# Opening of a transformer block on one core: block 0's chain first, four tokens to a partition, and block 1's query passes drawn between the opening's last steps

## Chip, cores and metric

The kernel runs on one core of one Trainium2 chip. The metric is the device time of an execution in microseconds. TensorE is PE in the profile (its weight loads PEld), VectorE is DVE, ScalarE is ACT, GpSimd is POOL; SyncE, which issues the transfers, is SP.

## What is computed

A pre-norm transformer block on x of 2048 tokens by 576 features: multi-query attention with 32 heads of 18 features and a single key and value head, then a gated bilinear feed-forward layer of 4608 features. All arrays are float32.

```python
def _A_ref(x, wq, wk, wv, wo):            # B, S, D = 1, 2048, 576; H, Dh = 32, 18
    q = (x @ wq).reshape(B, S, H, Dh).transpose(0, 2, 1, 3)
    k = x @ wk
    v = x @ wv
    scores = einsum("bhqd,bkd->bhqk", q, k) * (Dh ** -0.5)
    o = einsum("bhqk,bkd->bhqd", softmax(scores, axis=-1), v)
    return o.transpose(0, 2, 1, 3).reshape(B, S, H * Dh) @ wo
def _B_ref(x, w_gate, w_up, w_down):      # F = 4608
    return ((x @ w_gate) * (x @ w_up)) @ w_down
h = x + _A_ref(_layernorm(x), wq, wk, wv, wo)
out = h + _B_ref(_layernorm(h), w_gate, w_up, w_down)
```

## The kernel before

The 2048 tokens are four blocks of 512, each of four tiles of 128 tokens. Nearly every operand of PE is split in a high and a low part, and a product is the sum of three: high by high, high by low, low by high. A projection over 576 features is therefore 14 matmuls of 512 columns (`passes`), of which four need only the high parts and four the low part of x.

`keys_values` is the opening. It is written out by hand: the order of its lines is the order in each engine's queue. For every block it loads x, takes the layer norm's statistics (`stats`, DVE), makes scales (`scale`: an inverse root by three Newton steps on the engine it is given, `rstd`), normalises (`apply`, ACT), transposes on PE (`turn`: two PSUM tiles of the kind `ps_s` and a tail), and splits the transposed block into `XT` (`parts`: ACT casts the high part, DVE subtracts the low one). Then it projects keys, values and the last four query heads (`project`, tile `psk`), and writes keys to `kT` (`keys`) and values to `V` (`values`). For block 0 it also projects the other 28 query heads in four groups of seven (`query`, tile `psq`; `ready` splits and stores them in `q_dram`). `bound` and `bounds` make a row m for each head that bounds its scores from above: DVE's `tq` is the queries' size, `psg` the matmul, and m goes through `m_dram`. It is computed at first for group 0 alone, with `G0`.

Attention works in pairs. `pair` (L533, L534) is two score matmuls into one of the two `ps_s` tiles and one exponential on ACT, which makes P. `flush` (L538) adds two pairs' P times V into `acc`, one matmul for each of four heads. A step is two pairs and one flush; block 0 has 256 pairs, and each later block too. The transposes of the opening and the scores take turns in the same two `ps_s` tiles.

After `keys_values`, the loop in `run` draws the queries of blocks 1 to 3 (`queries`; one pass is one matmul of each of the two half-arrays `psq` and `psr`, L389) between the pairs at `RATE` = 1.9 a step, until none is left. `blocks` goes on: bare steps in which POOL and DVE split the output weights, steps with pieces of block 0's output projection (`outs`, tile `yo`, L689, three matmuls a piece, one or two pieces a step), the feed-forward layer of block 0 (`ffn`, L925) with pairs of later blocks between its matmuls, and so on. The places around the change:

```python
def apply(b, lo=0, hi=NQ):
    for s in range(lo, hi):
        ...
        act.activation(xh, xs[b][:, s, :], AF.Identity, bias=n, scale=r)
...
self.outs(2 if len(self.yos) > 1 else 1)
```

Of the kernel before, what the change touches and what calls it, by code (L numbers as in the profile page):

```python
# [54 lines left out]
class Block:  # L55
# [9 lines left out]

    def ps_s(self, name):
        return self.ps.tile([P, 2, TB], F32, tag="s", bufs=2, name=name)
# [34 lines left out]
    def rstd(self, var, name, eng=None, n=NQ):  # L102

        dve = eng or self.dve
        v = self.lp.tile([P, n], F32, tag="v", name=f"v{name}")
        t = self.lp.tile([P, n], F32, tag="t", name=f"t{name}")
        y = self.lp.tile([P, n], F32, tag="y", name=f"y{name}")
        yi = self.lp.tile([P, n], I32, tag="yi", name=f"yi{name}")
        dve.tensor_scalar(v, var, 1e-5, None, ALU.add)
        dve.tensor_copy(t, v.bitcast(I32))  # L110
        dve.tensor_scalar(yi, t, -0.5, 1597463007.0, ALU.mult, ALU.add)
        dve.tensor_scalar(v, v, -0.5, None, ALU.mult)
        g = yi.bitcast(F32)
        for _ in range(3):
            dve.tensor_tensor(t, g, g, ALU.mult)
            dve.tensor_tensor(t, t, v, ALU.mult)
            if eng is self.nc.gpsimd:
                eng.tensor_scalar(t, t, 1.5, None, ALU.add)
                eng.tensor_tensor(y, t, g, ALU.mult)
            else:  # L120
                dve.scalar_tensor_tensor(y, t, 1.5, g, ALU.add, ALU.mult)
            g = y
        return y
# [7 lines left out]
    def keys_values(self):  # L131
# [10 lines left out]
        wqr += [self.qb.tile([P, 5, 7 * DH], F32, tag="qs", bufs=QS, name=f"wqr{i}") for i in range(1, 4)]  # L142
        for b in range(NB):
            for s in range(NQ):
                sp.dma_start(xs[b][:, s, :], self.x[b * TB + s * P: b * TB + (s + 1) * P, :])
            if b == 0:
                sp.dma_start(self.C, self.cst)
                sp.dma_start(wkr, self.wkv)
                sp.dma_start(wqr[0], self.wq[cols[0]])
        for w, r in zip(cols[1:], wqr[1:]):  # L150
            sp.dma_start(r, self.wq[w])
# [19 lines left out]
        def scale(lo, hi, eng):  # L171
            r = self.rstd(mv[:, lo:hi, 1], f"a{lo}", eng, hi - lo)
            n = self.lp.tile([P, hi - lo], F32, tag=f"n{hi - lo}", name=f"n{lo}")
            pool.tensor_tensor(n, mv[:, lo:hi, 0], r, ALU.mult)
            pool.tensor_scalar(n, n, -1.0, None, ALU.mult)
            for j in range(lo, hi):
                rs[j] = r[:, j - lo:j - lo + 1], n[:, j - lo:j - lo + 1]

        def apply(b, lo=0, hi=NQ):
            for s in range(lo, hi):  # L180
                xh = xhs[s] = self.pp.tile([P, D], F32, tag="P", name=f"xh{b}_{s}") if b < 2 else xs[b][:, s, :]
                r, n = rs[NQ * b + s]
                act.activation(xh, xs[b][:, s, :], AF.Identity, bias=n, scale=r)

        def turn(b):

            tail = self.ps_m(f"trt{b}")
            for r in range(2):
                tr = self.ps_s(f"tr{b}_{r}").rearrange("p a (c q) -> p (a c) q", q=2 * P)
                for s in (2 * r, 2 * r + 1):  # L190
                    for c in range(4):
                        pe.transpose(tr[:, c, (s - 2 * r) * P:(s - 2 * r + 1) * P],
                                     xhs[s][:, c * P:(c + 1) * P], self.ident)
                trs.append((b, r, tr))
            for r, lo in ((P, 448), (64, 512)):
                for s in range(NQ):
                    pe.transpose(tail[:r, s * P:(s + 1) * P], xhs[s][:, lo:], self.ident)
            xhs.clear()
            trs.append((b, None, tail))

        def parts():

            while trs:
                b, r, tr = trs.pop(0)
                XT = self.XT[b]
                if r is None:
                    self.split_tail(XT[:, 8, :], tr)
                else:
                    sl = slice(2 * r * P, (2 * r + 2) * P)
                    self.split(XT[:, 0:4, sl], XT[:, 4:8, sl], tr)  # L210

        def project(b):
            psk = psks[b] = (self.ps_a if b < 2 else self.ps_f)(f"psk{b}")
            for i, (w, m) in enumerate(passes(w_h, w_l, self.XT[b])):
                pe.matmul(psk[:6 * DH], w, m, start=(i == 0), stop=(i == 13))

# [32 lines left out]
        def values(lo, hi):  # L249
            psv = (self.ps_m if lo else self.ps_a)(f"psv{lo}").rearrange("p (t c) -> p t c", c=64)  # L250
# [5 lines left out]
        def weights(i, cast):  # L256

            w, r = cols[i], wqr[i]
            cast(self.wq_h[w], r)
            pool.tensor_tensor(self.wq_l[w], r, f32(self.wq_h[w]), ALU.subtract)  # L260

        def query(i):
            psq = psqs[i] = self.ps_f(f"psq0_{i}")
            for k, (w, m) in enumerate(passes(self.wq_h[cols[i]], self.wq_l[cols[i]], self.XT[0])):
                pe.matmul(psq[:7 * DH], w, m, start=(k == 0), stop=(k == 13))  # L265
                yield

        def ready(i, copy):
# [4 lines left out]
            self.store_q(0, 7 * i, 7, qs, 0 if i else 4)  # L273
            yield
# [11 lines left out]
        q0, q1, q2, q3 = (query(i) for i in range(4))  # L286
        act.copy(w_h, wkr)
        stats(0, 4)
        scale(0, 4, dve)
# [7 lines left out]
        weights(1, act.copy)  # L297
        weights(2, pool.tensor_copy)
        stats(8, 12)
        scale(8, 12, pool)  # L300
        project(0)
        apply(1)
        some(q0, 4)
        turn(1)
        some(q0, 10)
        stats(12, 14)
        mean()
        parts()
        k0 = keys(0)
        some(k0, 2)  # L310
        some(q1, 7)
        g0 = bound(G0, 1)
        some(g0)
        some(q1, 5)
        t0 = ready(0, act.copy)
        some(t0)
        some(g0)
        some(t0)
        q = self.qt[0, 0] = self.qp.tile([P, 2, TB], F32R, tag="q", name="q0_0")
        apply(2, 0, 2)  # L320
        self.bounds(0, act.copy, self.pp.tile([H, 2, TB], F32R, tag="P", name="m2_0"), G0)
        some(k0)
        apply(2, 2, 4)
        self.load_q(q, 0, 0)
        self.load_m(q, 0, 0)
        stats(14, 16)
        scale(12, 16, pool)
        weights(3, pool.tensor_copy)
        project(1)
        turn(2)  # L330
        k1 = keys(1)
        some(k1, 2)
        parts()
        some(k1)
        some(q1, 3)
        values(0, 8)
        some(ready(1, dve.tensor_copy))
        step(q2, 4)
        step(q2, 3)
        apply(3)  # L340
        project(2)
        turn(3)
# [4 lines left out]
        some(q2, 15)  # L347
        some(ready(2, dve.tensor_copy))
        step()
        step()  # L350
        step()
        project(3)
        k3 = keys(3)
        some(k3, 3)
        step(q3, 7)
        g0 = bound(self.G, 4)
        some(g0, 2)
        step(q3, 8)
        some(ready(3, dve.tensor_copy))
        values(8, 16)  # L360


    def store_q(self, b, h0, n, qs, first=0):
# [4 lines left out]
        dve.scalar_tensor_tensor(tq[:r], f32(qs[:r, 0]), -1.0, f32(qs[:r, 0]), ALU.mult, ALU.max)  # L368
        rows = self.q_dram[b, h0 * DH:h0 * DH + r]
        for sl in (slice(0, first * DH), slice(first * DH, r)) if first else (slice(0, r),):  # L370
            sp.dma_start(rows[sl, 0:2, :], f32(qs[sl]))
            sp.dma_start(rows[sl, 2, :], f32(qs[sl, 0]))
        self.tqs.append((b, h0, n, tq))

# [5 lines left out]
    def queries(self, b):  # L380

        pe, act, dve, sp = self.pe, self.act, self.dve, self.sp
        for i, (h0, n) in enumerate(QT if b else ()):
# [3 lines left out]
            for k, (w, m) in enumerate(passes(w_h, w_l, self.XT[b])):  # L387
# [4 lines left out]
                if k == 5 and self.tqs and self.tqs[0][0] < b:  # L392
                    self.bounds(self.tqs[0][0])
# [6 lines left out]
            self.store_q(b, h0, n, qs)  # L400
            yield 2.5
        qs = self.qb.tile([P, 2, TB], F32R, tag="qs", bufs=QS, name=f"qs{b}_4")
        self.parts_q(4 * DH, qs, self.kvq[:4 * DH, b])
        self.store_q(b, 28, 4, qs)
        yield 0
        if b in (0, NB - 1):
            yield 4 if b else 7
            self.bounds(b)
# [243 lines left out]
    def load_wo_0(self, c):  # L652

        r = self.wo_r0[c] = self.w0.tile([P, D], F32, tag="wo_r", bufs=3, name=f"wo_r{c}")
# [176 lines left out]
    def down(self, b, pair):  # L831
# [4 lines left out]
        if pair == NC - 1:  # L836
# [23 lines left out]
            for s in range(NQ):  # L860
# [16 lines left out]
                sp.dma_start(self.out[b * TB + s * P: b * TB + (s + 1) * P, :], h[:, s, :])  # L877
# [102 lines left out]
    def load_x(self, b):  # L980
        h = self.h[b] = self.hp.tile([P, NQ, D], F32, tag="h", name=f"h{b}")
        for s in range(NQ):
            self.sp.dma_start(h[:, s, :], self.x[b * TB + s * P: b * TB + (s + 1) * P, :])
# [10 lines left out]
    def steps(self, on, work=iter(())):  # L994

        while on():
# [5 lines left out]
            self.outs(2 if len(self.yos) > 1 else 1)  # L1002
# [93 lines left out]
    def run(self):  # L1096
# [8 lines left out]
        with ExitStack() as st:  # L1105
# [11 lines left out]
            with tc.tile_pool(name="p0q", bufs=1) as self.p0q:  # L1117
# [4 lines left out]
                with tc.tile_pool(name="qb", bufs=2) as self.qb:  # L1122
                    self.keys_values()
                    def rest():
                        for b in range(NB):
                            yield from self.queries(b)
                    self.cast = self.dve.tensor_copy
                    others, live, due = rest(), True, 0.0
# [18 lines left out]
RATE = 1.9  # L1147
P_BUFS = 6
QS = 3
# [37 lines left out]
def passes(W, Wl, XT):  # L1187
# [4 lines left out]
    return r + [(W[:, 4], XT[:, 8]), (Wl[:, 4], XT[:, 8])]  # L1192

# [85 lines left out]
```

## Time and profile before

| | us |
|---|---|
| median of 3 runs (lowest, highest) | 2287.97 (2287.66, 2289.48) |
| the profiled execution | 2291.63 |
| its span, first to last instruction | 2289.8 |
| PE busy, DVE, ACT, POOL | 2263.5, 1175.7, 1443.3, 681.6 |
| first instruction on PE | 12.57 |
| first score matmul (pair 0) | 41.97 |
| first output piece of block 0 (pair 224) | 299.88 |

The mean granted clock of the span is 0.997. The page shows where engines are busy; the stages show where PE is not, or is at half clock; the timeline shows what a row waited for, in brackets behind it, with the idle time of its engine. A row's time is from its start to the end of its result, so rows of one engine overlap; what one costs its engine is the distance between starts.

### The profile page before, as it was taken

How to read it: one execution, taken by the hardware profiler on the slowest of the kernel's cores; microseconds unless marked ns; L12 is line 12 of the kernel's file. 1: busy time of each engine (PE TensorE's matmuls, PEld its weight loads, DVE VectorE, ACT ScalarE, POOL GpSimd, SP SyncE). 2: the span in 40 equal slices, each digit the busy share in tenths (PEclk: the TensorE clock that was granted, in tenths of full speed). 3: DMA queues.
4: the chain of work that ended last, by engine and by line, in shares of the span. 5: the costliest groups of instructions: out<-in, count | busy, mean ns of one | idle time of the engine just before them, and what ended most of it. 6: DMA issues, size and time to landing. Idle time of an engine off the chain costs nothing.

```text
span 2289.8 us, 45889 instructions
## 1 busy us (share of the span) xinstructions
PE 2263.5 (99%) x18090; PEld 1609.9 (70%) x18090; DVE 1175.7 (51%) x2134; ACT 1443.3 (63%) x1884; POOL 681.6 (30%) x862
## 2 busy tenths in 40 slices
PE   7999999999999999999999999999999999999998
PEld 5333345777777677677777777777777788888887
DVE  6332246565656576344444455444444476566665
ACT  5899977667676765767677767667677623232332
POOL 4000002545545454222222222222122233333342
PEclk9999999999999999999999999999999999999999
DMA  4212224433334443633333344634233355655553
GB/s 157 77 62 84 81 83 128 150 136 134 126 126 151 146 158 118 215 116 125 102 117 120 125 128 125 193 117 125 94 122 122 113 180 172 213 171 171 176 187 112
DMA packets 129434, 306.76 MB, mean 134 GB/s; under 512 B 17809, under 2 KB 17937, under 8 KB 129209
## 3 DMA queue, kind: packets, MB, share of 16 engines
q1 hardware_dynamic: 129209, 303.73, 40.7%
q8 instruction: 145, 2.38, 0.4%
q14 instruction: 80, 0.66, 0.1%
HBM read 233.76 MB, written 55.67 MB: 126 GB/s over the span
## 4 chain that ended last, share of the span: by engine, by line
PE 96%; ACT 1%; DVE 1%; issue 1%; DMA 1%; POOL 0%; SPq 0%; DVEq 0%; ACTq 0%; POOLq 0%
PE pg L925 21%; PE acc L538 20%; PE y L885 17%; PE gu L925 13%; PE s L533 12%; PE pu L925 5%; PE yo L689 3%; PE psq L389 2%; PE y L843 1%; ACT P L534 0%; PE psq L265 0%; DMA X<-X 0%; PE ye L843 0%; DVE XT L85 0%; PE tx L758 0%
## 5 line engine op out<-in xcount | busy, mean ns | idle before, releaser
L534 ACT ACTIVATE P<-s 128x1024 f32<-128x1024 f32 x1024 | 1024.9, 1026 | 271.1 <-PE s L533 195.0
L925 PE MATMUL pu<-X,ws 64*128 64x512 f32 x2592 | 702.2, 389 | 0.1
L925 PE MATMUL pg<-X,ws 64*128 64x512 f32 x2592 | 702.0, 389 | 0.0
L925 PEld LDWEIGHTS pg<-X,ws 64*128 64x128 f32 x2592 | 479.3, 185 | 67.8 <-issue 1.2
L538 PE MATMUL acc<-P,V 128*32 128x512 f32 x4096 | 488.8, 599 | 0.0
L925 PEld LDWEIGHTS pu<-X,ws 64*128 64x128 f32 x2592 | 477.1, 185 | 14.0 <-DVE h L690 1.0
L533 PE MATMUL s<-q,kT 56*128 56x512 f32 x2048 | 454.7, 422 | 4.4 <-ACT P L534 2.3
L885 PEld LDWEIGHTS y<-wdo,room 128*128 128x128 f32 x2856 | 386.0, 188 | 46.9 <-issue 44.2
L885 PE MATMUL y<-wdo,room 128*128 128x288 f32 x2856 | 402.8, 300 | 0.0
L892 ACT COPY tmp<-y 128x288 f32<-128x288 f32 x408 | 162.6, 399 | 330.1 <-PE y L885 311.3
L533 PEld LDWEIGHTS s<-q,kT 56*128 56x128 f32 x2048 | 210.7, 184 | 193.9 <-ACT P L534 116.0
L925 PE MATMUL gu<-X,ws 64*128 64x512 f32 x2592 | 301.6, 389 | 0.0
L893 POOL TENSOR_TENSOR x<-x,tmp 128x288 f32<-128x288 f32 x204 | 158.9, 809 | 434.4 <-ACT tmp L892 433.6
L538 PEld LDWEIGHTS acc<-P,V 128*32 128x32 f32 x4096 | 114.0, 109 | 243.1 <-issue 234.6
L925 PEld LDWEIGHTS gu<-X,ws 64*128 64x128 f32 x2592 | 249.7, 184 | 46.1 <-issue 4.6
L84 POOL CAST ws<-wr 128x1152 fp32r<-128x1152 f32 x144 | 171.7, 1193 | 322.4 <-PE pu L925 186.6
L893 POOL TENSOR_TENSOR h<-h,tmp 128x288 f32<-128x288 f32 x204 | 158.9, 806 | 344.8 <-ACT tmp L892 344.4
L85 DVE TENSOR_TENSOR ws<-wr,ws 128x1152 fp32r<-128x1152 f32 x144 | 198.6, 1379 | 74.6 <-POOL ws L84 74.6
L959 DVE TENSOR_TENSOR hf<-pu,g 128x512 f32<-128x512 f32 x96 | 66.4, 691 | 262.5 <-ACT g L955 259.1
L888 DVE TENSOR_TENSOR x<-x,y 128x288 f32<-128x288 f32 x272 | 117.2, 453 | 144.8 <-PE y L885 144.8
L888 DVE TENSOR_TENSOR h<-h,y 128x288 f32<-128x288 f32 x272 | 118.0, 454 | 111.9 <-PE y L885 109.0
L85 DVE TENSOR_TENSOR room<-S,room 128x1024 fp32r<-128x1024 f32 x68 | 86.3, 1270 | 146.5 <-ACT room L84 146.5
(170 smaller groups left out, 1628.2 us busy)
## 6 DMA issues: line engine op xcount, KB each, us to landing
wdo<-wd_dram SPq DMA_DIRECT2D x369, 288.0 KB
wr<-in_wgu_dram SPq DMA_DIRECT2D x144, 576.0 KB
wd_dram<-wdo SPq DMA_DIRECT2D x123, 288.0 KB
q<-q_dram SPq DMA_DIRECT2D x64, 216.0 KB
raw<-in_wd_dram SPq DMA_DIRECT2D x36, 288.0 KB
q_dram<-qs SPq DMA_DIRECT2D x15, 504.0 KB
X<-X SPq DMA_DIRECT2D x24, 256.0 KB
x<-in_x_dram SPq DMA_DIRECT2D x16, 288.0 KB
```

The costliest lines, as they stand in the source:

```text
L84: (copy or self.cast)(hi, src)
L85: self.dve.tensor_tensor(lo, src, f32(hi), ALU.subtract)
L533: self.pe.matmul(s_[:, i], self.kT[o:o + 56, t * P:(t + 1) * P], q[o:o + 56, pr], start=True, stop=True)
L534: self.act.activation(p_, s_, AF.Exp, scale=SCALE)
L538: self.pe.matmul(acc[32 * j:32 * j + 32, :], self.V[:, t, :], Ps[j // 2][:, j % 2, :], start=(t == 0), stop=(t == NT - 1), skip_group_chec ...
L689: pe.matmul(y[:, :HD], m, k, start=(i == 0), stop=(i == len(ms) - 1))
L885: pe.matmul(y[:, :HD], m[:, t * P:(t + 1) * P], k, start=(first and j == 0), stop=(j == 2), skip_group_check=True)
L888: dve.tensor_tensor(hs, hs, y[:, :HD], ALU.add)
L892: act.copy(z, y[:, :HD])
L893: pool.tensor_tensor(hs, hs, z, ALU.add)
L925: pe.matmul(ps, w[o:o + 64, wk, c], X[o:o + 64, xk, c], start=(j == 0), stop=(j == 26))
L959: dve.tensor_tensor(hf, pu, g, ALU.mult)
```

## The change

1. *Four tokens to a partition.* `tokens` gives a block of x or of the output as 128 partitions of four neighbouring tokens, instead of four tiles of 128 neighbouring tokens. A whole block of x can then be loaded with one transfer of 9216 bytes to a partition; block 0 comes in three pieces (one tile, one, two). Since keys, values, queries, residual and output use the same order, nothing else changes in the sums.
2. *Block 0's chain first.* The transfers are ordered x of block 0, constants, key weights, query weights 0 and 1, x of block 1, query weights 2 and 3, x of blocks 2 and 3. Their raw copies lie in the pool of the output weights (`wo_r`), not in `qs`. PE begins with 24 transposes of the identity into a tile that nobody reads (`WARM`). Block 0 is normalised half on DVE, half on ACT. Keys of block 0 and query group 0 come before block 1's transposes; block 1's normalising, which followed the scales, follows the bound's split. The statistics of later tiles are spread singly between DVE's other work.
3. *High parts first.* `highs_first` orders the 14 matmuls of a projection of the opening: high by high, low weights by high, high weights by low, tail.
4. *Passes of block 1 in the opening.* `others`, made before `keys_values`, is drawn at two passes in its last steps; the bound of block 0's other heads is made there too.
5. *Smaller edits.* The inverse root has one operation less; the mean's product is one DVE operation where the scale is made on DVE; `store_q` issues the first heads' store before `tq`; `outs(2)` always; later x comes in one transfer.

PE at the start, up to the first scores, before (`tr` and `trt` are transposes, `psk` keys, `psq_0` and so on query groups of block 0, `psb` and `psg` the bound, `psv` values):

```order
L215 MATMUL psk_312<-XT_100,wk 108x512 x14
L265 MATMUL psq_0_335<-XT_100,wq_h 126x512 x2
L265 MATMUL psq_0_335<-XT_100,wq_l 126x512
L265 MATMUL psq_0_335<-XT_100,wq_h 126x512
L192 MATMUL tr_0_341<-C,xh_0_327 128x128 x4
...
L416 MATMUL psg_0_431<-tq_0_421,G_148 32x512
L215 MATMUL psk_476<-XT_101,wk 108x512 x14
L192 MATMUL tr_0_492<-C,x_109 128x128 x8
...
L253 MATMUL psv_535<-C,kvq 128x44 x8
L533 MATMUL s_0_0_0_552<-q_0_427,kT 128x512 x2
```

And now:

```order
L307 MATMUL warm<-C 128x128 x24
...
L233 MATMUL psk_285<-XT_100,wk 108x512 x14
L284 MATMUL psq_0_302<-XT_100,wq_h 126x512 x4
L284 MATMUL psq_0_302<-XT_100,wq_l 126x512 x4
...
L476 MATMUL psg_0_355<-tq_0_340,G_138 32x512
...
L201 MATMUL tr_0_425<-C,xh_0_360 128x128 x4
...
L284 MATMUL psq_2_488<-XT_100,wq_h 126x512 x4
...
L233 MATMUL psk_503<-XT_101,wk 108x512 x14
L593 MATMUL s_0_0_0_530<-q_0_377,kT 128x512 x2
```

Block 1's transposes have moved from the middle of query group 0 to behind the bound; query group 2 stands ahead of the first scores, and block 2's transposes behind them.

DVE between block 0's scale and the subtractions of its transposed block, now (`bsa` and `mv` are statistics, x_108 is block 1's x; before, four tiles' statistics of block 1 stood here and no `xh`):

```order
L183 SCALAR_TENSOR_TENSOR n_198<-mv,ya_184 128x4
L192 TENSOR_SCALAR xh_0_200<-x_107,mv,ya_184 128x576
L192 TENSOR_SCALAR xh_1_202<-x_107,mv,ya_184 128x576
L103 BN_STATS bsa_0_236<-x_108 128x6 x2
L104 BN_AGGR mv<-bsa_0_236 128x2
L103 BN_STATS bsa_1_240<-x_108 128x6 x2
L104 BN_AGGR mv<-bsa_1_240 128x2
L89 TENSOR_TENSOR XT_100<-tr_0_209,XT_100 128x4x256
L89 TENSOR_TENSOR XT_100<-tr_1_218,XT_100 128x4x256
L98 TENSOR_TENSOR XT_100<-trt_227,XT_100 64x512
```

The subtractions wait behind statistics of two tiles of block 1, which need its x.

PE from block 3's transposes on, now (`s_0_2_0` is group 0, key tile 2, pair 0 of two; `psq_0_738` and `psr_0_739` are passes of block 1):

```order
L210 MATMUL trt_677<-C,x_109 64x128 x4
L284 MATMUL psq_3_550<-XT_100,wq_h 126x512 x3
L284 MATMUL psq_3_550<-XT_100,wq_l 126x512
L593 MATMUL s_0_2_0_719<-q_0_377,kT 128x512 x2
L593 MATMUL s_0_2_1_724<-q_0_377,kT 128x512 x2
L598 MATMUL acc_0_627<-P_0_1_0_618,V 32x512 x2
L598 MATMUL acc_0_627<-P_0_1_1_623,V 32x512 x2
L593 MATMUL s_0_3_0_733<-q_0_377,kT 128x512 x2
L445 MATMUL psq_0_738<-XT_101,wq_h 126x512
L445 MATMUL psr_0_739<-XT_101,wq_h 126x512
```

Before, the steps here held passes of block 0's groups 2 and 3, and the first pass of block 1 stood between the scores of pairs 20 and 21; now it stands between those of pairs 6 and 7. The first output piece stands behind pair 207 (before 223), and from the last output chunk, behind pair 261, PE's rows are the same in both. The core of the diff:

```diff
+    def tokens(self, dram, b):
+        return dram[b * TB:(b + 1) * TB, :].rearrange("(p s) d -> p s d", s=NQ)
...
-        dve.tensor_scalar(v, var, 1e-5, None, ALU.add)
+        dve.tensor_scalar(v, var, 1e-5, -0.5, ALU.add, ALU.mult)
...
+        for lo, hi in ((0, 1), (1, 2), (2, 4)):
+            sp.dma_start(xs[0][:, lo:hi], self.tokens(self.x, 0)[:, lo:hi])
+        sp.dma_start(self.C, self.cst)
+        sp.dma_start(wkr, self.wkv)
+        for i in range(2):
+            sp.dma_start(wqr[i], self.wq[cols[i]])
+        sp.dma_start(xs[1], self.tokens(self.x, 1))
...
+                if on is dve:
+                    dve.tensor_scalar(xh, xs[b][:, s, :], mv[:, NQ * b + s, 0:1], r, ALU.subtract, ALU.mult)
...
-        apply(0)
-        pool.tensor_tensor(w_l, wkr, f32(w_h), ALU.subtract)
-        weights(0, act.copy)
-        stats(4, 8)
-        scale(4, 8, pool)
-        turn(0)
-        parts()
...
+        warm = self.ps_a("warm")
+        for _ in range(WARM):
+            pe.transpose(warm[:, 0:P], self.ident, self.ident)
+        stats(0, 4)
+        highs(0, act.copy)
+        highs(1, act.copy)
+        scale(0, 4, dve)
+        apply(0, 0, 1, on=dve)
+        apply(0, 2, 3)
+        act.copy(w_h, wkr)
+        turns(0)
+        stats(4, 6)
+        parts()
...
+        drain(ready(3, dve.tensor_copy))
+        self.last_heads(0)
+        step()
+        step(others, 2)
+        drain(project(3))
...
-            self.outs(2 if len(self.yos) > 1 else 1)
+            self.outs(2)
...
+WARM = 24
...
+    p = passes(W, Wl, XT)
+    return p[0:12:3] + p[2:12:3] + p[1:12:3] + p[12:]
```

More of the change, by code (lines that the diff above doesn't have):

```diff
@@ L199, in turn, with turns, parts @@
             trs.append((b, None, tail))
-        def parts():
-            while trs:
+        def turns(b):
+            for r in range(2):
+                turn(b, r)
+            turn_tail(b)
+        def parts(n=3):
+            for _ in range(n):
                 b, r, tr = trs.pop(0)
@@ L212, in project @@
         def project(b):
-            psk = psks[b] = (self.ps_a if b < 2 else self.ps_f)(f"psk{b}")
-            for i, (w, m) in enumerate(passes(w_h, w_l, self.XT[b])):
+            psk = psks[b] = (self.ps_a if b < 2 else self.ps_m if b == NB - 1 else self.ps_f)(f"psk{b}")
+            for i, (w, m) in enumerate(highs_first(w_h, w_l, self.XT[b])):
                 pe.matmul(psk[:6 * DH], w, m, start=(i == 0), stop=(i == 13))
+                yield
         def mean():
@@ L331, in keys_values @@
+        some(t1)
+        stats(11, 12)
+        scale(8, 12, pool)
+        highs(3, pool.tensor_copy)
+        lows(3)
+        values(0, 4)
+        turns(1)
+        parts()
+        stats(12, 14)
+        scale(12, 14, pool)
+        some(q2, 15)
+        drain(project(1))
+        apply(2, 0, 1, 2, 3, on=dve)
         k1 = keys(1)
         some(k1, 2)
+        self.pair()
+        self.pair()
+        stats(14, 15)
+        t2 = ready(2, act.copy)
+        some(t2)
+        some(q3, 6)
+        turns(2)
@@ L333, in keys_values @@
         parts()
         some(k1)
[L335 to L342, printed above, removed]
+        some(q3, 4)
+        stats(15, 16)
+        scale(14, 16, dve)
+        step(q3, 0)
+        values(4, 8)
+        drain(project(2))
+        apply(3, 0, 1, on=dve)
+        apply(3, 2, 3)
+        drain(t1)
+        drain(t2)
+        turns(3)
         k2 = keys(2)
@@ L382, in queries @@
         pe, act, dve, sp = self.pe, self.act, self.dve, self.sp
-        for i, (h0, n) in enumerate(QT if b else ()):
+        for i, (h0, n) in enumerate(QT):
             r = n * DH
```

169 lines of the change are left out of this document (86 added, 83 removed).

## The prediction

> **What bounds the kernel now.** I read the page first, then the stages, then the opening row by row.
>
> ```profile
> PE 2263.5 (99%) x18090; PEld 1609.9 (70%) x18090; DVE 1175.7 (51%) x2134; ACT 1443.3 (63%) x1884; POOL 681.6 (30%) x862
> ```
>
> ```profile
> 0.00:42.00 42.00, 26.20 (x140) 20.73 (x140) 31.17 (x82) 23.47 (x32) 23.11 (x70) 1.00 0.59 192
> 42.00:85.00 43.00, 42.05 (x217) 20.84 (x221) 15.64 (x26) 28.55 (x33) 1.92 (x2) 0.88 0.24 78
> 85.00:140.00 55.00, 54.97 (x412) 20.58 (x404) 14.79 (x27) 50.76 (x53) 0.00 (x0) 1.00 0.21 68
> ...
> 40.00:42.00 2.00, 0.18 (x4) 0.09 (x2) 1.94 (x4) 0.15 (x1) 1.50 (x8) 0.94 0.44 127
> 42.00:44.00 2.00, 2.00 (x5) 1.38 (x6) 1.97 (x4) 1.02 (x1) 1.92 (x2) 0.50 0.01 2
> ...
> 50.00:52.00 2.00, 2.00 (x9) 1.38 (x6) 0.00 (x0) 2.00 (x4) 0.00 (x0) 0.50 0.00 0
> 52.00:54.00 2.00, 2.00 (x10) 1.51 (x9) 0.00 (x0) 0.54 (x1) 0.00 (x0) 1.00 0.00 0
> ```
>
> The columns after the stretch are PE, PEld, DVE, ACT, POOL, then the granted clock. From 85 us on PE is full, so time can only be won before that, or by less PE work, and the work stays. Before 85 us there are two holes. In the first stage PE works 26.2 of 42 us, and most of the rest is the wait for its first instruction at 12.57. In the second it counts as busy, but from 42 to 52 us at half clock, right after it had stood still for 1.8 us. The rows of the opening, in order of time:
>
> ```profile
> 6.57 0.82 DVE L99 BATCH_NORM_STATS2 bsa<-x 128x6 f32<-128x288 f32 x2 [0.81 <-DMA x<-in_x_dram]
> 8.43 0.64 ACT L287 CAST wk<-wkr 128x540 fp32r<-128x540 f32 x1 [6.42 <-DMA wkr<-in_wkv_dram]
> 8.59 0.17 DVE L109 TENSOR_SCALAR va<-mv 128x4 f32<-128x4 f32 x1
> 10.78 0.16 DVE L121 SCALAR_TENSOR_TENSOR ya<-ta,ya 128x4 f32<-128x4 f32 x1
> 11.65 3.15 ACT L183 ACTIVATE xh<-x,n,ya 128x576 f32<-128x576 f32 x4 [2.58 <-POOL n L175]
> 12.57 3.68 PE L192 MATMUL tr<-C,xh 128*128 128x128 f32 x16 [12.57 <-ACT xh L183]
> 16.04 1.92 PE L197 MATMUL trt<-C,xh 128*128 128x128 f32 x8
> 18.75 3.26 PE L215 MATMUL psk<-XT,wk 128*108 128x512 f32 x13 [0.56 <-DVE XT L85]
> ...
> 33.08 3.38 PE L215 MATMUL psk<-XT,wk 128*108 128x512 f32 x14
> 34.59 1.15 SPq L423 DMA_DIRECT2D m_dram<-m  x1
> 36.29 1.91 PE L192 MATMUL tr<-C,x 128*128 128x128 f32 x16
> 37.73 1.93 ACT L84 CAST XT<-tr 128x1024 fp32r<-128x1024 f32 x2
> 38.04 1.04 PE L197 MATMUL trt<-C,x 128*128 128x128 f32 x8
> 38.16 0.53 SPq L463 DMA_DIRECT2D q<-m_dram  x2
> 38.78 2.35 DVE L85 TENSOR_TENSOR XT<-tr,XT 128x1024 fp32r<-128x1024 f32 x2 [0.16 <-ACT XT L84]
> 41.97 0.89 PE L533 MATMUL s<-q,kT 56*128 56x512 f32 x2 [1.82 <-DVE XT L94]
> ```
>
> Eight tail transposes took 1.92 us at 16.04 (0.24 each) and 1.04 at 38.04 (0.11 from start to start), while the clock column says 1.00 for both: the first block's transposes run at half rate though no row of the clock admits it. A block's 24 transposes thus cost 2.6 us at full rate (36.29 to 38.83), its key projection 3.25 (14 matmuls from 33.08 to 36.29), and a query group of 14 of the same shape as much. These three are the bricks of the opening, and the order decides which of them wait.
>
> **The change, part by part.** I put its new order on these durations, engine by engine, and follow PE. Times below are us from the span's start, as in the rows.
>
> *To block 0's keys.* The third and fourth token tiles now come as one piece, so their statistics end near 8.75 instead of 8.56. The inverse root has 12 operations instead of 13 at 0.2 us: until 10.95; the mean's product moves from POOL to DVE (0.2): 11.15. Tiles 0 and 1 are normalised on DVE, 2 and 3 on ACT:
>
> ```profile
> L738 DVE TENSOR_SCALAR xh<-x,mvb,yb x4: 573/575/579, 358.8 to 360.3; 128x576 f32<-128x576 f32 x4
> ```
>
> DVE ends at 12.35, ACT (0.79 each, behind two weight casts) at 12.9 instead of 14.8. The 24 warm-up transposes start when the constants land (between 7.0 and the key weights' 8.43) and last 5.8 us at half rate, so they are over by 13 to 14; block 0's transposes follow at 0.11: until 16.0. ACT's two casts end at 15.9. DVE, however, first does the statistics of two tiles of block 1 (1.9 us; two took from 6.57 to 8.59 here), and x's second block now comes as one piece, so they wait for all of it. Its last byte is 3.44 MB down the queue; the kernel before moved
>
> ```profile
> DMA packets 2266, 3.49 MB, mean 291 GB/s; under 512 B 828, under 2 KB 956, under 8 KB 2266
> ```
>
> in its first 12 us: 11.8 us for 3.44 MB at that rate. With 1.3 us to land (my estimate; the upper bound is rival (a)) it is there at 13.1, DVE is free at 15.0, and its subtractions (1.2, 1.2, 0.7) end at 18.1. The lower bound, no wait at all, gains nothing beyond 0.2, since ACT's first cast ends at 15 too. The eight matmuls that need only ACT's high half now go first (16.0 to 17.9), the four with the low half follow DVE's second subtraction, the last two its third: keys done at 19.3 instead of 22.0 (18.75 + 3.26), and query group 0, which no longer yields to block 1's transposes, at 22.5.
>
> *To the first pair.* From 22.5 the chain is ACT's cast of group 0, then on DVE the subtraction, the copies for G and tq (0.6+0.7+0.4+0.7, with 0.5 of hand-overs): the bound's matmul psg runs at 25.4, beside it group 1 until 27.1. ACT and DVE split psg by 27.35, and its store is issued there instead of at 34.59. Only then does DVE normalise tiles 0 and 1 of block 1 (tq, psg's split and these stand in this order on DVE), so PE idles 0.65 us and transposes from 28.05 to 30.8. POOL's scales for it are ready by 25, starting behind the statistics at 20: 18 small operations took 5.0 us,
>
> ```profile
> 17.00 0.23 POOL L109 TENSOR_SCALAR va<-mv 128x4 f32<-128x4 f32 x1
> 21.76 0.23 POOL L175 TENSOR_SCALAR n<-n 128x4 f32<-128x4 f32 x1
> ```
>
> and there are 17 now. Query group 2 (to 34.05) covers DVE's splits of block 1, which end at 34.5; block 1's keys end at 37.3. The m load follows its store by 3.6 us (34.59 to 38.16) and landed within 3.8 (by 41.97), so it is there at 34.8 at the latest. So the first pair is scored at **37.3 instead of 41.97**, with query group 2 done in place of block 2's transposes.
>
> *To pair 14.* PE's own work from there, with the step prices of the next fence: two transposed blocks 5.2, keys of blocks 2 and 3 6.5, query group 3 3.25, 14 pairs at 0.33 (4.6), six acc groups at 1.0, 8 passes at 0.23 (1.9), and psv, psb and psg 2.35: 29.8. Its waits, from laying ACT's and DVE's rows beside it: transposes and scores take turns in the same two banks, so block 2's transposes wait 0.5 for P0 and P1; pairs 2 and 3 wait 1.1 for DVE's splits of block 2; pairs 4 and 5 wait 1.8 for those of block 3, which stand on DVE behind two tq and the keys' two operations; a pass waits 0.4 for its bank, and 0.2 goes elsewhere: 4.0. Their bounds are 0 (rival (f)) and twice as much. Pair 14 begins at 37.3+33.8 = **71.1**. No single wait is longer than 1.0, against the 1.8 that went ahead of the slow clock, so I count no half-clock stretch.
>
> *From there.* Before begins pair 21 at 84.28 with no pass drawn; this kernel begins pair 14 with 8 passes drawn.
>
> ```profile
> 84.28 0.40 PE L533 MATMUL s<-q,kT 56*128 56x512 f32 x2
> 86.75 1.06 PE L538 MATMUL acc<-P,V 128*32 128x512 f32 x8
> 88.86 1.06 PE L538 MATMUL acc<-P,V 128*32 128x512 f32 x8
> ...
> 61.51 3.77 ACT L534 ACTIVATE P<-s 128x1024 f32<-128x1024 f32 x4 [0.40 <-PE s L533]
> ...
> 299.88 1.05 PE L689 MATMUL yo<-wo,oT 126*128 126x288 f32 x6
> 300.86 0.73 PE L533 MATMUL s<-q,kT 56*128 56x512 f32 x4
> 301.52 1.07 PE L538 MATMUL acc<-P,V 128*32 128x512 f32 x8
> 302.51 1.05 PE L689 MATMUL yo<-wo,oT 126*128 126x288 f32 x6
> 303.50 0.73 PE L533 MATMUL s<-q,kT 56*128 56x512 f32 x4
> ...
> 347.63 3.08 PE L689 MATMUL yo<-wo,oT 126*128 126x288 f32 x18
> 350.64 0.73 PE L533 MATMUL s<-q,kT 56*128 56x512 f32 x4
> ```
>
> A step is two pairs. With two output pieces it takes 2.64 (300.86 to 303.50): scores 0.66, acc 0.99, pieces 0.99. With two passes it takes 2.11 (86.75 to 88.86), so a pass is 0.23. Bare it is 1.65 on PE but 1.88 on ACT (four P in 3.77), and ACT holds it. Before needs 215.6 us from pair 21 to the first output piece (299.88, pair 224). This kernel's first piece stands at pair 208: 97 steps, 4.5 fewer (7.5 us), and 8 passes fewer (1.9): 206.2. From there to 350.64, four pieces into the last chunk at pair 262, before needs 50.8. This kernel runs 16 steps with two pieces (42.3), 11 bare ones held by ACT (20.9), and four pieces (2.0): 65.2. That place comes at 71.1+206.2+65.2 = 342.5, **8.1 us earlier**; behind it both have the same PE rows, and PE is full.
>
> At no cost: the whole-block loads of x for blocks 2 and 3, hidden behind a block's feed-forward work (if that cover were gone, the 1.18 MB would cost about 4 us at 291 GB/s); the output rows, equally long and only farther apart, of which the last 128 alone lie behind PE's end (I take 0, half a microsecond either way); one operation fewer in each later inverse root, beside a full PE.
>
> **The time.** The profiled execution (2291.63 us, span 2289.8) would become 2283.5. The median is 3.66 below it and loses the same: 2287.97 - 8 = **2280.0**.
>
> **Rivals.** (a) *Block 1's x lands late.* DVE stands before it, and PE behind DVE, 1:1. At the 192 GB/s that the first stage's row ends with, instead of 291, 3.44 MB take 17.9 us: 4.8 lost, 2285. For it: one 1.18 MB piece behind two weight loads of short rows, and nothing of it can be used before its last byte. Against: 3.49 MB in 12 us. 0.10.
> (b) *The transposes do not raise the clock*, so block 0's stay at 0.24 and its first matmuls too: 3.2 on the transposes, 0.8 on the keys, 2284. The trace speaks against: half rate until 17.7, full at 18.75, with one matmul between. 0.06. The Trainium skill, "TensorE: Matmul & The Clock Gate", section "Part 4: PE-mode transpose", says so: transposes do not count as busy for the clock gate. This trace disagrees, by those two rows; by the page the time would be 2284.
> (c) *One half-clock stretch comes back*, at the waits near 44 or 54 us: 10.4 us at half rate, 5.2 lost, 2285. For it: two waits of 0.9 stand close together there. 0.08.
> (d) *Slower:* the clock halves at all three waits (39, 44, 54) and each stretch lasts 10.4 us: 15.6 lost, 2295.6. It is slower than before from 16 us at half clock on. Before, the clock fell only once, and the stage from 85 us, with waits of its own for P, shows 1.00. 0.05.
> (e) *The gain is given back at the end of block 0's pairs*, because the 11 bare steps are not held by ACT at 1.88 but take as long as steps with two pieces, 2.64: 8.4 lost, 2288. For it: they hand over between ACT and PE twice a step. Against: the four P in a row at 0.94. 0.05.
> (f) *Fewer waits than I count:* the 4.0 vanish as DVE's splits are done earlier: 2276. 0.10.
>
> **How the numbers follow.** The forecast has 0.56 and covers 2277 to 2283 (waits of 2 to 6 us instead of 4.0, x landing a microsecond sooner or later). The measurement can tell about 0.2%, 4.6 us, from no change: faster is under 2283.4. The forecast, (f) and half of (a) and of (b) are faster: 0.74; the other halves, (c) and (e) lie within: 0.21; (d) is slower: 0.05. The range 2274 to 2286 takes in (a), (b), (c), (f) and 2 us below (f) for what else overlaps better than I laid it out; it leaves out (d) and (e), 0.10.
>
> **What would show it.** Block 0's tail transposes at 0.11; DVE's first XT subtraction at 15 (later: (a)); keys 0 done near 19.3; the first score near 37; clock 1.00 from 40 to 70 (0.50: (c), (d)); waits under 1 us for XT subtractions before pairs 2 to 5; pair 14 at 71; the last chunk's first pieces at 342, and the rest shifted alike. A gain at pair 14 that has gone at 342 would prove my ACT and PE step prices wrong.

## The result, and the profile after

The changed kernel takes **2293.21 us** (median of 12 runs, 2291.9 to 2294.27), the kernel before 2288.88 in the same comparison (12 runs, 2286.94 to 2292.33): a ratio of 1.002 with a 95% interval from 1.0012 to 1.0028, some 4 us slower. The forecast was 2280. The profiled execution took 2291.9 us (span 2290.4), against 2291.63 (2289.8) before.

The opening, however, went nearly as worked out. Its stages and its rows, in order of time:

```profile
0.00:42.00 42.00, 34.31 (x187) 27.62 (x187) 35.58 (x88) 20.74 (x29) 24.17 (x64) 1.00 0.65 213
42.00:85.00 43.00, 40.84 (x272) 19.39 (x271) 22.66 (x49) 31.36 (x35) 0.27 (x2) 1.00 0.27 89
```

```profile
6.28 5.11 PE L307 MATMUL warm<-C 128*128 128x128 f32 x24 [6.28 <-DMA C<-in_cst_dram]
11.22 1.91 PE L201 MATMUL tr<-C,xh 128*128 128x128 f32 x16
12.10 0.82 DVE L103 BATCH_NORM_STATS2 bsa<-x 128x6 f32<-128x288 f32 x2 [0.69 <-DMA x<-in_x_dram]
12.97 1.04 PE L210 MATMUL trt<-C,xh 128*128 128x128 f32 x8
14.01 2.30 DVE L89 TENSOR_TENSOR XT<-tr,XT 128x1024 fp32r<-128x1024 f32 x2
14.49 3.52 PE L233 MATMUL psk<-XT,wk 128*108 128x512 f32 x14 [0.49 <-ACT XT L88]
25.95 0.29 SPq L483 DMA_DIRECT2D m_dram<-m  x1
35.79 0.74 PE L593 MATMUL s<-q,kT 56*128 56x512 f32 x4
43.27 0.50 PE L593 MATMUL s<-q,kT 56*128 56x512 f32 x2 [0.64 <-DVE XT L89]
52.88 0.49 PE L593 MATMUL s<-q,kT 56*128 56x512 f32 x2 [0.56 <-DVE XT L89]
54.01 0.49 PE L593 MATMUL s<-q,kT 56*128 56x512 f32 x2 [0.64 <-DVE XT L89]
70.52 0.50 PE L593 MATMUL s<-q,kT 56*128 56x512 f32 x2
276.94 1.05 PE L750 MATMUL yo<-wo,oT 126*128 126x288 f32 x6
343.81 0.74 PE L593 MATMUL s<-q,kT 56*128 56x512 f32 x4
```

The reader is to see PE busy 8.1 us more of its first 42 us (34.31, before 26.20; 4.9 of these are the warm-up transposes, from 6.28 to 11.22, whose result nobody reads), the first pair at 35.79 (before 41.97), and the place that was at 350.64 now at 343.81. So 6.8 us have been won there against the profile of before. Now the two feed-forward (FFN) stages, each line with the shortest, median and longest duration in ns and the first and last start; `pg` is made while pairs are drawn between the FFN's matmuls, `gu` after the last pair. Before:

```profile
L925 PE MATMUL pg<-X,ws x2592: 383/388/501, 366.2 to 1822.1; 64*128 64x512 f32 x200
L925 PE MATMUL gu<-X,ws x2592: 383/386/497, 1826.2 to 2276.0; 64*128 64x512 f32 x200
```

After:

```profile
L986 PE MATMUL pg<-X,ws x2592: 383/392/502, 359.4 to 1821.7; 64*128 64x512 f32 x200
L986 PE MATMUL gu<-X,ws x2592: 383/386/502, 1825.9 to 2276.2; 64*128 64x512 f32 x200
```

The lead is 6.8 us at the first `pg` and 0.3 at the first `gu`. PE runs the same matmuls in the same order between them and is as full: it is busy 1198.93 of the 1200 us from 500 to 1700, and was 1198.79 before. That stage, before and after:

```profile
500.00:1700.00 1200.00, 1198.79 (x9875) 873.01 (x9875) 608.74 (x1088) 826.57 (x1064) 388.47 (x472) 1.00 0.42 135
500.00:1700.00 1200.00, 1198.93 (x9833) 860.21 (x9833) 601.96 (x1077) 823.31 (x1061) 385.75 (x469) 1.00 0.41 134
```

The median `pg` has become 4 ns longer (388 to 392), the median `gu` has not changed. I call the time from the first `pg` to the first `gu` the **FFN stretch**: 1459.95 us before, 1466.46 after, 6.5 more. The lead falls all along it: 4.2 us at the thousandth `pg`, 2.2 at the 1600th, 1.0 at the 2300th. Behind it another 0.9 goes, and the span ends 0.6 us later than before.

### The profile page after: what moved, and what is told of

Read it like the earlier page. It is cut to its first block, busy times and chain, and to the rows that moved or that the text cites. A ratio compares the mean times of both kernels' runs of the same rounds, so it can differ in the third digit from the quotient of the medians.

```text
span 2290.4 us, 45926 instructions
## 1 busy us (share of the span) xinstructions
PE 2268.7 (99%) x18114; PEld 1599.6 (70%) x18114; DVE 1180.3 (52%) x2152; ACT 1436.5 (63%) x1877; POOL 681.3 (30%) x856
## 4 chain that ended last, share of the span: by engine, by line
## 5 line engine op out<-in xcount | busy, mean ns | idle before, releaser
L594 ACT ACTIVATE P<-s 128x1024 f32<-128x1024 f32 x1024 | 1024.0, 1026 | 271.4 <-PE s L593 189.6
```

Of the source, the lines that this page charges most:

```text
L594: self.act.activation(p_, s_, AF.Exp, scale=SCALE)
```

## The experiments

**First round: banks and addresses.** The warm-up is the first to take a PSUM tile, so the tags' banks changed (a tag names the tiles that share buffers); the raw query weights made the `wo_r` buffers longer, so X and the FFN weights moved in SBUF. That gives two theories of what made the FFN stretch longer, banks and addresses; the new token order is a third. In the changed kernel:

```diff
-        warm = self.ps_a("warm")
+        warm = self.ps_m("warm")
```

> The changed kernel with one word altered: the warm-up's tile is taken from the tag m instead of the tag a. Tags get their PSUM banks in the order of first use, so the accumulator goes back to bank 5 and m to bank 0, as before the change; every instruction stays in its place. From the first FFN matmul to the last both profiles have the same matmuls, but the changed kernel's lead of 6.8 us shrinks evenly to 0.1 us while pairs are drawn between the FFN's matmuls: from the start of one pu to the start of the next it takes 233 ns in the median where before it took 227. Theory banks (the even loss comes from the bank of a tag): 227 ns again, the lead kept, about 6.7 us less than the changed kernel, 2286.5 us. Theory addresses (it comes from the 736 bytes by which the change moves X, the weights and all behind them in SBUF): 233 ns, 2293.2 us as the changed kernel. Theory transfers (whole-block loads and stores of four tokens to a partition): 233 ns, 2293.2 us.

In the kernel before:

```diff
+        warm = self.ps_a("warm")
+        pe.transpose(warm[:, 0:P], self.ident, self.ident)
+        warm = self.ps_s("warm_s")
+        pe.transpose(warm[:, 0, 0:P], self.ident, self.ident)
         act.copy(w_h, wkr)
```

> The kernel before with two transposes of the identity put first, one into the tag a and one into the tag s: the accumulator then lies in bank 0 and m in bank 5, as in the changed kernel. Nothing else moves. Theory banks: the pu to pu step goes from 227 to 233 ns and the kernel is about 6.7 us slower than before, 2295.6 us. Theory addresses and theory transfers: 227 ns and 2288.9 us, within 0.5 us.

In the kernel before, and in the changed one (its `wqr` buffers alike):

```diff
-        r = self.wo_r0[c] = self.w0.tile([P, D], F32, tag="wo_r", bufs=3, name=f"wo_r{c}")
+        w = self.w0.tile([P, 5, 7 * DH], F32, tag="wo_r", bufs=3, name=f"wo_r{c}")
+        r = self.wo_r0[c] = w.rearrange("p a b -> p (a b)")[:, 0:D]
```

> The kernel before with its three wo_r buffers enlarged from 2304 to 2520 bytes a partition, as in the changed kernel, their use unaltered: X, the weights and everything behind them in SBUF lie 672 bytes higher, X at 103488 (a multiple of 64, as the changed kernel's 103552; before 102816, half way between two). Theory addresses: pu to pu 233 ns and about 2295.6 us. Theory banks and theory transfers: 227 ns and 2288.9 us.

```diff
-        w = self.w0.tile([P, 5, 7 * DH], F32, tag="wo_r", bufs=3, name=f"wo_r{c}")
-        r = self.wo_r0[c] = w.rearrange("p a b -> p (a b)")[:, 0:D]
+        w = self.w0.tile([P, 656], F32, tag="wo_r", bufs=3, name=f"wo_r{c}")
+        r = self.wo_r0[c] = w[:, 0:D]
```

> The changed kernel with wo_r buffers of 2624 bytes: X and everything behind it lie exactly 1024 bytes above their place before the change, so their position within any power of two up to 1024 bytes is that of before. Theory addresses: pu to pu 227 ns and about 2286.5 us. Theory banks and theory transfers: 233 ns and 2293.2 us.

Both theories fell: the FFN stretch was 1466.18 (banks of before), 1460.24 (banks of after), 1460.38 (X shifted) and 1466.76 us (X put back). Neither edit by itself carried the loss from one kernel to the other.

**Second round: the whole layout, the transfers, the warm-up.** The first run puts the banks, the bank parity (which of its two banks a `pg` gets) and the SBUF addresses back at once, X and all behind it exactly 1024 bytes above their old place (the `wo_r` edit above, `warm` from `m`, one more `ps_f` tile, a pad of 64 bytes behind `wo_r`, and `n` as in the third round); the second gives the kernel before the new token order; the third gives the changed kernel the old one; the fourth sets `WARM = 1`.

> The changed kernel with the whole memory layout of before at once: PSUM tags in the banks of before and in step with them (pg and pu in the same bank for every matmul), every SBUF tile up to the wo_r buffers at its old address, X and all behind it 1024 bytes above the old one. Two transposes of the identity and one memset of 64 bytes are added for it in the opening. Measure: from the start of the first pg matmul to the start of the first gu matmul, 1459.95 us before, 1466.46 changed, though PE's instructions between them are the same. Theory layout (banks and addresses act only together): 1460 us and a median of about 2287. Theory transfers (four tokens to a partition) and theory clock history (before, and its two variants, had a stretch of half clock at 42 us, the changed kernel and its two variants none): 1466.5 us and 2293.2.

> The kernel before with four tokens to a partition in its loads of x and its stores, in as many transfers as before. Theory transfers: pg to gu takes 1466.5 us and the kernel 2295. Theories layout and clock history: 1460 us and 2288.9.

```diff
-        return dram[b * TB:(b + 1) * TB, :].rearrange("(p s) d -> p s d", s=NQ)
+        return dram[b * TB:(b + 1) * TB, :].rearrange("(s p) d -> p s d", s=NQ)
```

> The changed kernel with the rows of before, token by token down the partitions, in the same transfers: x is then read, and the output written, in rows of 2304 bytes. Theory transfers: pg to gu takes 1460 us and the kernel about 2287, or more by what the opening's loads lose. Theories layout and clock history: 1466.5 us and 2293.2.

> The changed kernel with one transpose of warm-up instead of 24. I expect stretches of half clock in the opening, block 0's transposes at 0.21 us instead of 0.11, and the first pair 1 to 4 us later. Theory clock history (PE, once it has been throttled in the opening, runs the pair-mixed FFN steps at the faster pace, or is throttled by what came before): pg to gu 1460 us, and a median of about 2289 for all the later opening. Theories layout and transfers: 1466.5 us and a median of 2294 to 2297.

The layout did it. With the whole layout of before:

```profile
L989 PE MATMUL pg<-X,ws x2592: 385/388/501, 360.9 to 1817.8; 64*128 64x512 f32 x200
L989 PE MATMUL gu<-X,ws x2592: 383/386/498, 1821.9 to 2272.2; 64*128 64x512 f32 x200
```

The median `pg` is 388 again, the stretch 1461.04 us, the time 2287.69 us (10 runs). The token order has no part in it (1460.73 in the kernel before, 1466.08 in the changed one). Nor has the clock history: this run's clock is 1.00 throughout its opening, and its stretch is short. The run with one warm transpose (1466.21) was to test that too, but had no half clock either. Its opening shows what the warm-up does:

```profile
13.31 3.68 PE L201 MATMUL tr<-C,xh 128*128 128x128 f32 x16 [4.21 <-DVE xh L192]
16.78 1.25 PE L210 MATMUL trt<-C,xh 128*128 128x128 f32 x8
18.09 3.51 PE L233 MATMUL psk<-XT,wk 128*108 128x512 f32 x14
```

Sixteen transposes take 3.47 us from start to start (0.22 each) where 24 others ahead of them made it 1.75 (0.11, the rows 11.22 and 12.97 above), and the first pair comes at 39.06 instead of 35.79. Not all of these 3.3 us are the warm-up's: in this profile block 0's second tile of x landed later (its statistics start at 8.20 instead of 5.86), and so the transposes began 2.1 us later. It also shows that transposes alone raise the pace: at 17.21 us their step falls from 0.21 to 0.11 us, before PE has run a matmul of any other kind. I expected a stretch of half clock in the clock's own rows as well; there was none. The time of that kernel, 2293.53 us, cannot be told from that of the changed one.

**Third round: 64 bytes.** What the layout run had and the first round had not is the bank parity, and a line that the change did not touch:

```diff
-            n = self.lp.tile([P, hi - lo], F32, tag=f"n{hi - lo}", name=f"n{lo}")
+            n = self.lp.tile([P, NQ], F32, tag="n4", name=f"n{lo}")[:, 0:hi - lo]
```

The changed kernel makes two scales of two tiles each, so this line makes a second tag, `n2`, whose two buffers take 64 bytes ahead of x, `q`, P and all that follows. The other two runs put 64 unused bytes there in the kernel before, and take one more `ps_f` tile in the changed one.

> The changed kernel with one line altered: the small tile n of the layer norm's scale always has four columns and one tag, as before the change, where the changed kernel has a second tag for the scales of two. The second tag's two buffers take 64 bytes, and by these every tile behind them (x, q, P, the outputs, room) lies 64 bytes higher than before: P's first buffer at 40256, not 40192. Banks stay as in the changed kernel, X lies 672 bytes above its old place. Theory 64 bytes (one of these tiles sets the pace): from the first pg to the first gu 1460 to 1461 us (before 1459.95, changed 1466.46, whole layout of before 1461.04), median 2287.5. Theory parity (pg and pu have changed banks against s): 1466.3 us and 2293.3. Theory several (only banks, parity and addresses together): between, or 1466.3.

> The kernel before with an unused tile of 64 bytes in the layer norm's pool, so that every tile behind it lies 64 bytes higher, as in the changed kernel; one memset is added, nothing else. Theory 64 bytes: pg to gu 1466.3 us and a median of about 2295. Theories parity and several: 1460 us and 2289.

> The changed kernel with one transpose of the identity into a tile of the tag f ahead of the queries, so that every later pg and pu is in the bank that it had before the change, 6 for 7 and 7 for 6. Theory parity: pg to gu 1460 us and 2287. Theory 64 bytes: 1466.3 us and 2293.2.

In the kernel before with 64 bytes more:

```profile
L926 PE MATMUL pg<-X,ws x2592: 383/393/501, 361.5 to 1828.6; 64*128 64x512 f32 x200
L926 PE MATMUL gu<-X,ws x2592: 383/386/522, 1832.7 to 2282.9; 64*128 64x512 f32 x200
```

It takes 2298.33 us, 1.0039 (1.0025 to 1.0053) of the kernel before: an unused tile of 64 bytes costs 9 us, more than its theory had (a stretch of 1471.26 us instead of 1466.3). In the changed kernel, one tag for `n` brings the stretch from 1466.46 to 1461.68 and the time to 2288.72. Parity alone does nothing (1466.57, 2292.59).

**Fourth round: which tile.** All on the changed kernel with `n` in one tag, with unused tiles at the head of one or two pools, like this:

```diff
         p0 = self.op
+        pool.memset(self.pp.tile([P, 16], F32, tag="pad", bufs=1, name="pad"), 0.0)
```

> The changed kernel with n in one tag (1461.7 us from the first pg to the first gu) and 64 unused bytes put directly ahead of P: q stays at 32000, P begins at 40256, and all behind it lies where it does in the changed kernel. Theory P (P, or a tile behind it, sets the pace): 1466.5 us and 2293. Theory q (the tile q that the s matmuls read): 1461.7 us and 2288.

> The same with the 64 bytes behind P: q at 32000 and P at 40192 as before the change, the outputs ob and os, oT and room, X and all the rest as in the changed kernel. Theory room (the tiles behind P set the pace): 1466.5 us and 2293. Theories P itself and q: 1461.7 us and 2288.

> 64 bytes ahead of q and 64 more ahead of P: q begins at 32064, P and all behind it 128 bytes above their place with n in one tag. Theory q: 1466.5 us and 2293. Theories P and room, if a shift by 128 bytes is none: 1461.7 us and 2288.

> 128 bytes ahead of all: q at 32128, P at 40320, room at 77600, X at 103616. Theory multiples of 128 (a tile counts as shifted only by what is left over 128 bytes): 1461.7 us and 2288. Theory any shift (distances to the unmoved tiles kT and V count): 1466 us or more and 2293.

`q` alone off by 64 bytes, then everything off by 128:

```profile
L988 PE MATMUL pg<-X,ws x2592: 383/392/502, 360.8 to 1822.4; 64*128 64x512 f32 x200
L988 PE MATMUL gu<-X,ws x2592: 383/386/503, 1826.6 to 2277.0; 64*128 64x512 f32 x200
```

```profile
L987 PE MATMUL pg<-X,ws x2592: 383/388/501, 359.6 to 1817.5; 64*128 64x512 f32 x200
L987 PE MATMUL gu<-X,ws x2592: 383/386/502, 1821.8 to 2271.6; 64*128 64x512 f32 x200
```

From P on, these two kernels have every tile at the same address (bytes from the start of a partition). `q` lies at 32064 or at 32128: 1465.79 or 1462.21 us, 2292.53 or 2288.61. What else differs is x and the layer norm's small tiles ahead of `q`, 128 bytes apart; no `pg`, `pu` or `s` matmul reads them. With P and all behind it, or the outputs, `room` (the FFN's work space) and all behind them, where the changed kernel has them, but `q` at 32000, it stays low (1462.80 and 1463.44).

**Fifth round: the same in the kernel before,** with pads ahead of `q` and of P (64 and 64 bytes, then 32 and 96).

> The kernel before with 64 unused bytes ahead of q and 64 ahead of P: q at 32064, P and all behind it 128 bytes higher, so only q is off the multiple of 128. Theory q (the tile that the s matmuls read slows the FFN matmuls drawn behind them when it does not begin on a multiple of 128 bytes): from the first pg to the first gu 1466 to 1471 us, median 2294 to 2298, as with 64 bytes ahead of everything (1471.26, 2298.33). Theory several (q together with another tile off the multiple): under 1463 us and 2290.

> The same with q at 32032, 32 bytes off, all behind it as in the run with q alone 64 bytes off. Theory multiples of 128 and theory multiples of 64: as with q 64 off, or slower, 1466 us or more. Theory multiples of 32 (only the half of 128 bytes is bad): 1460 to 1462 us and 2289.

```profile
L927 PE MATMUL pg<-X,ws x2592: 385/391/503, 362.9 to 1825.2; 64*128 64x512 f32 x200
L927 PE MATMUL gu<-X,ws x2592: 383/386/497, 1829.4 to 2279.5; 64*128 64x512 f32 x200
```

```profile
L927 PE MATMUL pg<-X,ws x2592: 383/392/501, 363.3 to 1829.7; 64*128 64x512 f32 x200
L927 PE MATMUL gu<-X,ws x2592: 383/386/498, 1833.8 to 2283.9; 64*128 64x512 f32 x200
```

Moving `q` by 64 bytes makes the stretch 1466.45 us and the time 2295.17 (1.0025, interval 1.0014 to 1.0037); by 32 bytes, 1470.56 and 2299.49 (1.0044, 1.0027 to 1.0061). All 17 runs and the two kernels, by where `q` begins:

| `q` begins | kernels | FFN stretch, us | median `pg`, ns | medians of the time, us |
|---|---|---|---|---|
| 32000 (250 x 128), opening of before | before; banks; X shifted; four tokens | 1459.95 to 1460.73 | 386 to 388 | 2288.7 to 2289.8 |
| 32000 or 32128, opening of after | whole layout; `n` in one tag; P on; outputs on; all 128 | 1461.04 to 1463.44 | 386 to 388 | 2287.7 to 2289.5 |
| 32064, opening of after | changed; banks; X put back; token order; one warm; parity; `q` alone | 1465.79 to 1466.76 | 390 to 392 | 2292.5 to 2293.8 |
| 32064, opening of before | 64 bytes ahead of all; `q` alone | 1471.26; 1466.45 | 393; 391 | 2298.3; 2295.2 |
| 32032, opening of before | `q` alone | 1470.56 | 392 | 2299.5 |

Each stretch is that of one profile. Kernels with the same addresses in it differ by up to 0.8 us (before and four tokens, 1459.95 and 1460.73), so smaller differences say nothing.

## Why the prediction was wrong

**The steps up to the last chunk held.** The prediction had block 1's x at 13.1 (12.10; that 1.3 us of the 13.1 are for landing no run shows by itself), the first subtraction at 15.0 (14.01), keys 0 done at 19.3 (about 18.0), the bound's store at 27.35 (25.95), the first pair at 37.3 (35.79), pair 14 at 71.1 (70.52), the first output piece at 277.3 (276.94), and the place before pair 262 at 342.5 (343.81). The waits before pairs 3, 4 and 5 were the named ones, for DVE's splits, and 0.56 to 0.64 us long; the clock stayed at 1.00. Of the 8.1 us forecast there, 6.8 came; the opening gave more than worked out (from 41.97 to 35.79 at the first pair, not to 37.3), the way behind it less: from pair 14 to the place before pair 262 it took 273.3 us, not 271.4. The first is in part luck: in the eleven profiles of this opening with 24 warm transposes the first pair comes at 35.8 to 37.8, 36.8 in the mean, and this one is the earliest. The second is nearly all one term that was too small, the 20.9 us for 11 bare steps, which begin at the first and third of these rows and end at the second and fourth:

```profile
308.78 0.50 PE L593 MATMUL s<-q,kT 56*128 56x512 f32 x2
319.14 1.06 PE L750 MATMUL yo<-wo,oT 126*128 126x288 f32 x6
329.76 0.50 PE L593 MATMUL s<-q,kT 56*128 56x512 f32 x2
342.00 1.88 PE L750 MATMUL yo<-wo,oT 128*128 128x288 f32 x12
```

Five of them take 10.36 us and six 12.24, 22.6 in all: 2.05 a step, not 1.88, with a wait for ACT in every second one. That is rival (e) in small, 1.7 us of its 8.4. Two slips of the working changed little: 11 steps at 1.88 are 20.7, and (a)'s 4.8 us leave out the 1.3 for landing. The transposes did raise PE's pace, and block 0's took 0.11 us each, so rival (b) is out. The Trainium skill, "TensorE: Matmul & The Clock Gate", section "Part 4: PE-mode transpose", says that the full clock does not engage for transposes, which do not count as busy in the same way; the run with one warm transpose, 0.21 us falling to 0.11 with only transposes run, speaks against that.

**The failed step is "behind it both have the same PE rows, and PE is full".** Both halves are true, and the conclusion that the gain stays does not follow: the same rows on a full PE ran 6.5 us longer, 3.6 to 4.8 of them because `q` had moved by 64 bytes. None of the rivals had it; (e), a gain given back, looked for it in block 0's pairs and in the wait for ACT, and the order and the work were all that I compared. The cause is shown from both sides: `q` put back on a multiple of 128 takes 3.6 us (all 128 against `q` alone) to 4.8 us (`n` in one tag, which moves the tiles behind `q` back too) out of the changed kernel's stretch, and `q` moved off it puts 6.5 (64 bytes) or 10.6 us (32 bytes) into that of before.

**A second step failed: "The median is 3.66 below it and loses the same".** The profiled execution of before had 10.24 us of half clock in its opening. Six other profiles of that opening, in the variants of before, had 6.8, four times 3.4, and in one case none; of the one with four tokens, this is the stage that holds it (the number behind POOL's is the granted clock; it was 0.50 for the same 4 us in the profile before):

```profile
42.00:46.00 4.00, 4.00 (x11) 2.07 (x11) 2.15 (x3) 2.45 (x3) 1.55 (x2) 0.57 0.53 172
```

Their first `pg` comes at 361.5 to 365.9 us, 363.3 in the mean, not at 366.2; in the 11 profiles of the new opening with 24 warm transposes it comes at 359.3 to 361.3, 360.3 in the mean. So the opening wins about 3 us in a usual execution, and the one I measured it against was the worst of seven. Three won, 6.5 lost in the FFN stretch and 0.9 behind it make 4.4 us slower; measured are 4.3.

**What the change is worth with `q` in place.** With `n` in one tag it is 0.9993 (0.9984 to 1.0003) of the kernel before, not to be told from it; with the whole layout of before 0.9989 (0.998 to 0.9999), 2287.69 us: the best version here, about 2 us faster than before and, across two comparisons, 5.5 faster than the change as it was made. The 3 us of the opening are not all kept, since the stretch stays 1.1 to 3.5 us above that of before even so.

**Open.** Why the tile that the `s` matmuls read shows in the `pg` and `pu` matmuls drawn behind them, no run here shows. The traces say where: a step from one `pu` to the next with no pair between takes 227 to 231 ns in the median with `q` on a multiple of 128, and 231 to 235 off it, if it is one of the first three behind a pair; the 48 or 49 that stand farther off take 227 in all 19 kernels. Whether `s` itself slows can't be told (medians 388 to 392 ns on a multiple, 390 to 399 off it). Open too is what the 1.1 to 3.5 us are: 1461.04 with all as before, 1461.68 with X elsewhere, 1463.44 with outputs, room and X elsewhere. And in the kernel before, 64 bytes ahead of all make 1471.26 where `q` alone makes 1466.45; which of the other tiles adds 4.8 us no run here shows. An offset of 96 bytes was not tried.

## What to carry to other kernels

When a change makes, drops or resizes any tile, compare the addresses of the tiles that PE reads in its long stages, not only the order of its instructions: a 64-byte tile in an early pool can cost more than a rewritten opening wins, and a pad is a quick trial. A "full PE with the same rows" is not the same time; compare the median duration of its commonest matmul in both traces. And before a stage of a few us is priced against one profiled execution, look whether its clock row is typical, since a stretch of half clock there differed by 10 us between profiles of the same opening.

## What was not expected of the hardware

- The tile `q`, which the `s` matmuls stream, at a multiple of 128 bytes in SBUF, or 32 or 64 bytes off it: 386 to 388 or 390 to 393 ns for the median FFN matmul drawn between those that read it, with no wait in the trace, and 0.2 to 0.4% of the kernel. Where no pairs are drawn, `gu`, the median was 386 in every run. It is no rule for every streamed tile: X, which `pg` itself streams, begins at 102816 in the kernel before, 32 bytes off a multiple of 128, and at 103552, a multiple, in the slower changed one.
- With `q` on a multiple of 128, other layout shifts cost less: P and all behind it by 64 bytes 1.1 us of 1460, the outputs, room and all behind them 1.8. X and all behind it by 672 bytes (0.4) and an exchange of PSUM banks (0.3) stay within the 0.8 us by which profiles of the same addresses differ.
